# Two half loads of x0 at the heads of the load queues: a change in the first microseconds of a gated attention and FFN kernel

## The chip, the cores and the metric

The kernel runs on 1 core of one Trainium2 chip. The metric is the device time in microseconds (us) of one execution; before the change it is 288.54 us, the median of 3 runs (288.52 to 288.88).

## The reference

For 2048 tokens of width 640 the kernel computes a linear attention branch a and a SwiGLU branch b, and mixes them by a gate of each token. Cut to what matters:

```python
g = sigmoid((x * gate_w).sum(-1, keepdims=True))        # one number for each token
q, k, v = split((x @ wqkv))                             # 32 heads of 20
phi(t) = concat(softmax(t @ w_phi), softmax(-(t @ w_phi)))
kv = sum_s phi(k)[s] outer v[s];  z = sum_s phi(k)[s]
a = ((phi(q) @ kv) / (phi(q) @ z + 1e-6)) @ wo
b = (silu(x @ w_gate) * (x @ w_up)) @ w_down
out = g * a + (1 - g) * b
```

All inputs and the output are bf16.

## The kernel before

The tokens are cut into 16 tiles of 128 (x0 to x15). TensorE needs every x tile transposed, with the 640 features on the partitions in 5 chunks of 128: `xT[:, t, c, :]`. Tiles 0 to 3 are loaded plainly into `xs` and transposed by TensorE; the others are loaded transposed by the DMA engines.

**Two orders written out by hand** drive the build. `LOADS` is the order in which the input DMAs are issued; each has a fixed issuing engine, SP or ACT (ScalarE), and each of the two has a queue of its own that takes them in order. `ORDER` is the order of the work items. The items at the start are:

- `H` (`warm`): a pair of dummy matmuls, 128x128 by 128 columns, on a constant of ones. Nothing reads their results; they wait for no load.
- `X t` (`xpose`): five TensorE transposes of x tile t, and DVE copies of the results into `xT`. For t below 3 there are two copies: chunk 0 (128x128) as soon as the first transpose is done, then chunks 1 to 4 (128x512).
- `G` (`gcol`): TensorE transposes the gate row `gwr` (5 rows of 128) into one column for each chunk, and DVE copies the five columns into column 640 of `wvg`, so that the v matmuls give the gate's dot product as well.
- `U t.c` (`vpart`): the two matmuls (320 and 321 columns) of chunk c of the v projection of tile t, from `xT[:, t, c, :]` and the weight rows `wvg[:, c, :]` (load `w c`). The second one reads column 640, so `U0.0` needs x0's first copy, the weight load w0 and the gate column.
- `V`, `F`, `M`, `K` and so on: the rest. It all follows behind on TensorE in the written order.

Before the change the work starts with thirteen pairs of dummies `H0` to `H12`, then `X0 G X1 U0.0 U1.0 U0.1 X2 U1.1`, and so on. The queues start with: SP: x0, gate row, w1, w2, w3, and the first FFN columns; ACT: w0, x1, x2, x3, w4, and w_phi.

**PSUM** is used as four pairs of banks; `next_pair` takes the least recently used pair that isn't held. An item that writes a pair waits for the reads of what was there.

**Waits** are made by `_Tracker`. For each access it forms keys (space, first byte, end byte) in `keys_of`, and `run` makes an instruction or DMA wait for the last writer and, where it writes, for all readers of every key that overlaps its own, unless its engine is known to have waited already. The key comes from the column part of the access:

```python
        for s in ap.tensor.shape[1:]:
            row *= s
        size = mybir.dt.size(ap.dtype)
        dims = [(step, n) for step, n in list(ap.ap)[1:] if n > 1]
        off = ap.offset % row
```

Here `row` is the number of elements of one partition, and `dims` leaves out the first dimension of the access, which is that of the partitions. Before the change every tile of `xs` is written by one DMA over all 128 partitions. A DMA waits on the engine that issues it; what stands behind it on that engine's queue is issued afterwards.

Of the kernel before, what the change touches and what calls it, by code (L numbers as in the profile page):

```python
# [6 lines left out]
P = 128  # L7
# [23 lines left out]


LOADS = """
x0 w0 x1 g w1 x2 w2 x3 w3 w4 f0 h k0 k1 t4 k2 k3 k4 t5 t6 t7 t8 t9 t10 t11 t12 t13 t14 t15 q0 q1 q2 q3
q4 f1 f2
"""

ORDER = """
H0 H1 H2 H3 H4 H5 H6 H7 H8 H9 H10 H11 H12 X0 G X1 U0.0 U1.0 U0.1 X2 U1.1 U2.0 U0.2 U1.2 U2.1
X3 U2.2 U0.3 U1.3 U2.3 U0.4 U1.4 U2.4 V3 Y F0.1 M1 i3 M0 F0.0 M2 V4 M3 M4 K0 K1 I S0 V6 V5 S1 P0  # L40
K3 K2 P1 E0 V9 K4 E1 S3 V7 P3 K5 S2 V8 V10 S4 P2 P4 E2 R0 E3 K6 S5 P5 S6 i4 E4 V14 K7 K8 P6 V15 S7
R2 E5 K9 S8 P7 R1 E6 K10 S9 V12 P8 E7 P9 K11 S10 P10 F0.2 R3 F1.2 E8 E9 K12 E10 S11 S12 K14 S14
# [11 lines left out]
class _Tracker:  # L54
# [90 lines left out]
    def run(self, eng, fn, reads=(), writes=(), dma=False):  # L145
        rkeys = list(dict.fromkeys(k for a in reads for k in self.keys_of(a)))
        wkeys = list(dict.fromkeys(k for a in writes for k in self.keys_of(a)))
        need = {}

        def req(ev, raw):  # L150
            if ev is None:
                return
            s, v = ev
            if s == eng and not dma and (eng == "pe" or not raw):
                return
            if v > need.get(s, 0):
                need[s] = v

        for k in rkeys:
            for kk in self._conflicts(k):  # L160
                req(self.lastw[kk], True)
                if k[0] == "psum":
                    for s, v in self.readers[kk].items():
                        req((s, v), False)
        for k in wkeys:
            for kk in self._conflicts(k):
                req(self.lastw[kk], True)
                for s, v in self.readers[kk].items():
                    req((s, v), False)
        self._wait(eng, need)  # L170
        ins = fn()
        if dma:
            sn = "d%d" % self.ndma
            self.ndma += 1
            self._add_sem(sn)
            inc = 16
        else:
            sn, inc = eng, 1
        ins.then_inc(self.sem[sn], inc)
        self.cnt[sn] += inc  # L180
        v = self.cnt[sn]
        snap = dict(self.known[eng])
        if not dma:
            snap[sn] = max(snap.get(sn, 0), v)
        self.evknow.setdefault(sn, {})[v] = snap
        ev = (sn, v)
        for k in wkeys:
            self.lastw[k] = ev
            self.readers[k] = {}
        for k in rkeys:  # L190
            r = self.readers[k]
            if r.get(sn, 0) < v:
                r[sn] = v
        return ev


def _build(nc, A_x, A_wqkv, A_w_phi, A_wo, B_x, B_w_gate, B_w_up, B_w_down, gate_w, out):
    tr = _Tracker(nc)
    pe, act, dve, pool, sp = nc.tensor, nc.scalar, nc.vector, nc.gpsimd, nc.sync
# [53 lines left out]
    def at(name, shape, dtype, rel):  # L253
        n = mybir.dt.size(dtype)
        for s in shape[1:]:
            n *= s
        assert rel + n <= SLAB, (name, rel + n, SLAB)
        t = nc.alloc_sbuf_tensor_at(name, list(shape), dtype, offset=sbase + rel)
        tr.reg(t, "sbuf", sbase + rel)
        return t  # L260
# [4 lines left out]
    xs = at("xs", [P, NPE, D], BF16, 10752)  # L265
# [5 lines left out]
    gwr = at("gwr", [P, P], BF16, 30656)  # L271
# [72 lines left out]
    def dma(e, dst, src, transpose=False):  # L344
        eo = tr.eng[e]

        def fn():
            if transpose:
                return eo.dma_start_transpose(dst, src)
            return eo.dma_start(dst, src)  # L350
        rd = [src] if src.tensor.name in tr.base else []
        wr = [dst] if dst.tensor.name in tr.base else []
        return run(e, fn, rd, wr, dma=True)
# [4 lines left out]
            channel_multiplier=cm), [ap], [ap])  # L358


    XQ = ["sp", "act", "act", "act"]
    WQ = ["act", "sp", "sp", "sp", "act"]
    x2 = A_x[0]
    out2 = out[0]

    def load_rows(e, dst, c, c0):
        return dma(e, dst, A_wqkv[c * P:(c + 1) * P, c0:c0 + D])

    def load_x(t):
        dma(XQ[t], xs[:, t, :], x2[t * P:(t + 1) * P, :])  # L370

    def load_xt(t):
        dma("sp", xT[:, t, :, :], x2[t * P:(t + 1) * P, :], transpose=True)
# [7 lines left out]
    def load_wv(c):  # L381
        wv_evs.append(load_rows(WQ[c], wvg[:, c, 0:D], c, 2 * D))

    def load_gate():
        dma("sp", gwr[0:5, :], bass.AP(gate_w.tensor, gate_w.offset, [[P, 5], [1, P]]))

    def load_phi():
        tr._wait("act", dict([wv_evs[3]]))
# [12 lines left out]
    H0 = [0, 6, 12, 19, 25]  # L401
    H1 = [7, 13, 20, 26, 32]
# [342 lines left out]
    def kv_end():  # L745
# [6 lines left out]
        "H": lambda i: warm(), "i": fills, "X": xpose, "G": gcol, "U": vpart, "V": vtile,  # L752
        "M": lambda m: premult(1, m), "R": lambda m: premult(0, m),
        "K": ktile, "S": knorm, "P": kmul, "p": lambda t: kmul(t, "dve"), "E": kvtile, "x": load_x, "t": load_xt, "w": load_wv, "g": load_gate, "h": load_phi, "k": lambda m: load_wt(1, m), "q": lambda m: load_wt(0, m),
        "f": lambda i: load_ffn(FCUT[i], FCUT[i + 1]), "L": load_late_weights, "T": tail_weights, "J": gates,
        "Y": w_blocks, "I": kv_begin, "N": kv_end, "Z": z_row,
# [8 lines left out]
def bass_gated_mix__linear_kernel_hedgehog__swiglu_ffn__prompt_kernel(  # L765
    nc: bass.Bass,
    A_x: bass.AP,
    A_wqkv: bass.AP,
    A_w_phi: bass.AP,
    A_wo: bass.AP,  # L770
    B_x: bass.AP,
    B_w_gate: bass.AP,
    B_w_up: bass.AP,
    B_w_down: bass.AP,
    gate_w: bass.AP,
    out: bass.AP,
):
    _build(nc, A_x, A_wqkv, A_w_phi, A_wo, B_x, B_w_gate, B_w_up, B_w_down, gate_w, out)
# [28 lines left out]
```

## Time and profile before

| | before |
|---|---|
| median of 3 runs | 288.54 us (288.52 to 288.88) |
| the profiled execution | 288.52 us |
| its span, from the first to the last instruction | 287.3 us |
| PE (TensorE matmuls) busy | 284.5 us, 99% |
| PEld (weight loads) busy | 174.7 us, 61% |
| DVE, ACT, POOL busy | 163.4, 151.9, 159.9 us |

The 1.2 us between the profiled execution's time and its span lie outside the instructions. Matmuls are pipelined, so a duration in the profile is one matmul's passage through the array, and the distance between two starts is its cost in a dense stream. "L296" is line 296 of the kernel; the v matmuls, the FFN and the projections are all issued there, the transposes at L308, the dummies at L478, the DVE copies at L320, plain DMAs at L350 and transposing ones at L349. "SPq" and "ACTq" are DMA issues on the two engines; the time of such a row is that of the issue, and the DMA lands later.

### The profile page before, as it was taken

To read this page: it belongs to the slowest core of one execution; us is meant where nothing else is said; L and a number is where in the kernel's file an instruction comes from. 1 tells how busy PE (TensorE), PEld (TensorE's weight loads), DVE (VectorE), ACT (ScalarE), POOL (GpSimd) and SP (SyncE) were. 2 spreads that over 40 slices of the span, in tenths; PEclk is the share of its full clock that TensorE was granted. 3 is DMA by queue.
4 is the path that set the end of the run, shared out by engine and by line. 5 is a ranking of instruction groups with operands and counts; after the bars stand their busy time and mean duration, and the time that the engine had idled before them with its cause. 6 is when DMAs were issued, how large, how long until landed. Compare 5 with 4: busy or idle time off the path is not lost.

```text
span 287.3 us, 4960 instructions
## 1 busy us (share of the span) xinstructions
PE 284.5 (99%) x1975; PEld 174.7 (61%) x1975; DVE 163.4 (57%) x243; ACT 151.9 (53%) x252; POOL 159.9 (56%) x125
## 2 busy tenths in 40 slices
PE   8999999999999999999999999999999999999997
PEld 7667777675644545557775556675554446656776
DVE  2337748576569978589991565970317899000000
ACT  0767778576775566682535653225586552234112
POOL 8286999879446789836542438350754558501000
PEclk9999999999999999999999999999999999999999
DMA  7975797000010598202573002061020006210101
GB/s 236 200 117 120 114 292 257 3 1 2 2 47 0 130 283 162 50 2 50 68 155 73 3 1 50 2 155 37 2 50 0 3 1 123 52 46 0 49 23 48
DMA packets 48944, 21.62 MB, mean 75 GB/s; under 512 B 39384, under 2 KB 48792, under 8 KB 48920
## 3 DMA queue, kind: packets, MB, share of 16 engines
q1 hardware_dynamic: 47400, 20.43, 31.2%
q10 hardware_dynamic: 1520, 0.87, 1.0%
q8 instruction: 16, 0.26, 0.4%
q14 instruction: 8, 0.07, 0.1%
HBM read 9.29 MB, written 2.62 MB: 41 GB/s over the span
## 4 chain that ended last, share of the span: by engine, by line
PE 99%; DVE 0%; issue 0%
PE ps L296 97%; PE ps L478 1%; PE ps L308 1%; DVE osb L733 0%
## 5 line engine op out<-in xcount | busy, mean ns | idle before, releaser
L324 POOL TENSOR_TENSOR hT<-hT,us 128x512 bf16<-128x512 bf16 (+1 forms) x56 | 65.1, 1175 | 65.3 <-DVE hT L328 47.0
L328 DVE SCALAR_TENSOR_TENSOR hT<-hT,ps 128x512 bf16<-128x512 bf16 (+1 forms) x56 | 37.4, 682 | 67.0 <-ACT hT L314 53.3
L296 PE MATMUL ps<-xT,wg 128*128 128x512 bf16 x260 | 64.6, 379 | 0.0
L296 PE MATMUL ps<-xT,wu 128*128 128x512 bf16 x260 | 64.6, 379 | 0.0
L296 PE MATMUL ps<-wd,hT 128*128 128x320 bf16 (+2 forms) x462 | 63.9, 295 | 0.0
L324 POOL TENSOR_TENSOR ph<-eq,qc 128x1320 bf16<-128x1320 bf16 x16 | 42.4, 2648 | 25.6 <-DVE qc L638 20.8
L296 PEld LDWEIGHTS ps<-wd,hT 128*128 128x128 bf16 x462 | 44.5, 98 | 17.4
L296 PE MATMUL ps<-wqk,xT 128*128 128x320 bf16 x320 | 47.7, 299 | 0.0
L314 ACT ACTIVATE hT<-ps 128x512 bf16<-128x512 f32 (+2 forms) x60 | 35.7, 596 | 16.7 <-PE ps L296 16.5
L296 PEld LDWEIGHTS ps<-xT,wu 128*128 128x128 bf16 x260 | 25.4, 98 | 30.7
L314 ACT ACTIVATE us<-ps 128x512 bf16<-128x512 f32 (+1 forms) x56 | 33.5, 598 | 19.2 <-PE ps L296 18.2
L314 ACT ACTIVATE osb<-ps,omg 128x640 bf16<-128x640 f32 (+2 forms) x17 | 12.9, 758 | 55.7 <-PE ps L296 55.7
L296 PEld LDWEIGHTS ps<-xT,wg 128*128 128x128 bf16 x260 | 25.0, 98 | 27.8 <-ACT oT L314 0.8
L324 POOL TENSOR_TENSOR ekr<-ekr,krec 128x1280 bf16<-128x1280 bf16 x16 | 37.4, 2358 | 5.8 <-DVE krec L338 5.8
L296 PEld LDWEIGHTS ps<-wqk,xT 128*128 128x128 bf16 x320 | 30.5, 98 | 13.1 <-issue 0.4
L314 ACT ACTIVATE eq<-ps 128x640 bf16<-128x640 f32 x32 | 22.4, 704 | 20.8 <-POOL ph L324 10.7
L335 DVE TENSOR_REDUCE ksum<-ekr 128x64 f32<-128x1280 bf16 x16 | 23.5, 1470 | 11.7 <-ACT ekr L314 11.7
L314 ACT ACTIVATE ekr<-ps 128x640 bf16<-128x640 f32 x32 | 22.3, 704 | 8.7 <-PE ps L296 8.2
L335 DVE TENSOR_REDUCE qz<-eq 128x64 f32<-128x1280 bf16 x16 | 23.7, 1478 | 2.6 <-ACT eq L314 2.6
L296 PE MATMUL ps<-wog,oT 128*128 128x320 bf16 (+2 forms) x165 | 24.7, 294 | 0.0
L296 PE MATMUL ps<-wvg,xT 128*128 128x320 bf16 (+1 forms) x160 | 24.1, 299 | 0.0
L335 DVE TENSOR_REDUCE qw<-ez 128x64 f32<-128x1280 bf16 x16 | 23.6, 1476 | 0.0
(73 smaller groups left out, 189.4 us busy)
## 6 DMA issues: line engine op xcount, KB each, us to landing
out_dram<-osb SPq DMA_DIRECT2D x15, 160.0 KB, 1.9
wd<-in_B_w_down_dram SPq DMA_DIRECT2D x1, 2080.0 KB, 9.6
wg<-in_B_w_gate_dram SPq DMA_DIRECT2D x1, 1040.0 KB, 10.6
wu<-in_B_w_up_dram SPq DMA_DIRECT2D x1, 1040.0 KB, 12.8
wg<-in_B_w_gate_dram SPq DMA_DIRECT2D x1, 800.0 KB, 5.8
wu<-in_B_w_up_dram SPq DMA_DIRECT2D x1, 800.0 KB, 8.3
wog<-in_A_wo_dram SPq DMA_DIRECT2D x2, 375.0 KB, 7.1
xs<-in_A_x_dram ACTq DMA_DIRECT2D x3, 160.0 KB, 3.6
```

The lines of the kernel that those rows point to most:

```text
L296: last = pe.matmul(o, lhsT=l, rhs=r, start=st, stop=sp_, skip_group_check=sk)
L308: last = pe.transpose(o, i, ident[0:k, 0:k])
L314: return run("act", lambda: act.activation(o, i, func, scale=scale), rd, [o])
L324: return run(e, lambda: eo.tensor_tensor(o, a, b, op), [a, b], [o])
L328: return run("dve", lambda: dve.scalar_tensor_tensor(out=o, in0=a, scalar=s, in1=b, op0=op0, op1=op1), rd, [o])
L335: return run("dve", lambda: dve.tensor_reduce(o, i, AX.X, ALU.add), [i], [o])
L478: last = pe.matmul(bank(2 * pr, 0, P), lhsT=c, rhs=c, start=True, stop=True)
```

## The change

x0 is loaded by two DMAs of 64 rows each, the first issued by SP and the second by ACT, each as the first of its queue. The gate row goes behind the second half on ACT; w0 goes behind the first half on SP. In `ORDER`, the thirteen pairs of dummies in front of `X0` become ten; two pairs stand between `G` and `U0.0`, `X1` follows `U0.0` and no longer precedes it, and one pair stands between `X1` and `U1.0`.

```diff
 LOADS = """
-x0 w0 x1 g w1 x2 w2 x3 w3 w4 f0 h k0 k1 ...
+x0 g w0 x1 w1 x2 w2 x3 w3 w4 f0 h k0 k1 ...
 ORDER = """
-H0 H1 H2 H3 H4 H5 H6 H7 H8 H9 H10 H11 H12 X0 G X1 U0.0 U1.0 U0.1 X2 U1.1 ...
+H0 H1 H2 H3 H4 H5 H6 H7 H8 H9 X0 G H10 H11 U0.0 X1 H12 U1.0 U0.1 X2 U1.1 ...
-    XQ = ["sp", "act", "act", "act"]
-    WQ = ["act", "sp", "sp", "sp", "act"]
+    WQ = ["sp", "sp", "sp", "sp", "act"]
     def load_x(t):
-        dma(XQ[t], xs[:, t, :], x2[t * P:(t + 1) * P, :])
+        parts = [("sp", 0, 64), ("act", 64, P)] if t == 0 else [("act", 0, P)]
+        for e, p0, p1 in parts:
+            dma(e, xs[p0:p1, t, :], x2[t * P + p0:t * P + p1, :])
     def load_gate():
-        dma("sp", gwr[0:5, :], bass.AP(gate_w.tensor, gate_w.offset, [[P, 5], [1, P]]))
+        dma("act", gwr[0:5, :], bass.AP(gate_w.tensor, gate_w.offset, [[P, 5], [1, P]]))
```

More of the change, by code (lines that the diff above doesn't have):

```diff
@@ L33 @@
 LOADS = """
-x0 w0 x1 g w1 x2 w2 x3 w3 w4 f0 h k0 k1 t4 k2 k3 k4 t5 t6 t7 t8 t9 t10 t11 t12 t13 t14 t15 q0 q1 q2 q3
+x0 g w0 x1 w1 x2 w2 x3 w3 w4 f0 h k0 k1 t4 k2 k3 k4 t5 t6 t7 t8 t9 t10 t11 t12 t13 t14 t15 q0 q1 q2 q3
 q4 f1 f2
@@ L38 @@
 ORDER = """
-H0 H1 H2 H3 H4 H5 H6 H7 H8 H9 H10 H11 H12 X0 G X1 U0.0 U1.0 U0.1 X2 U1.1 U2.0 U0.2 U1.2 U2.1
+H0 H1 H2 H3 H4 H5 H6 H7 H8 H9 X0 G H10 H11 U0.0 X1 H12 U1.0 U0.1 X2 U1.1 U2.0 U0.2 U1.2 U2.1
 X3 U2.2 U0.3 U1.3 U2.3 U0.4 U1.4 U2.4 V3 Y F0.1 M1 i3 M0 F0.0 M2 V4 M3 M4 K0 K1 I S0 V6 V5 S1 P0
```

## The prediction

> **What bounds the kernel now.** I read the chain that ended last first, in order of time, because it says where a delay at the start would go.
>
> ```profile
> 12 pieces in order of time: start us, us, what
> 0.84 2.93 PE ps L478 x26
> 3.77 1.32 PE ps L308 x11
> 5.09 0.98 PE ps L296 x6
> 6.08 0.28 PE ps L308 x5
> 6.36 1.37 PE ps L296 x10
> ...
> 77.46 207.92 PE ps L296 x1271
> ```
>
> The chain is TensorE from the first dummy to the last matmul. No later piece is a wait for a load or another engine, so there is no slack behind the start: what the first v matmul loses, the end loses. It also works the other way, so the first 6 us are read instruction by instruction in the timeline:
>
> ```profile
> 0.80 0.40 SPq L350 DMA_DIRECT2D xs<-in_A_x_dram  x1
> 0.82 0.41 ACTq L350 DMA_DIRECT2D wvg<-in_A_wqkv_dram  x1
> 0.84 2.93 PE L478 MATMUL ps<-const-bfloat16-1.0 128*128 128x128 bf16 x26 [0.84 <-PEq L792]
> 1.25 1.42 ACTq L350 DMA_DIRECT2D xs<-in_A_x_dram  x3
> 3.76 0.45 PEld L308 LDWEIGHTS ps<-ident,xs 128*128 128x128 bf16 x5 [0.25 <-DMA xs<-in_A_x_dram]
> 3.76 0.72 PE L308 MATMUL ps<-ident,xs 128*128 128x128 bf16 x5
> 4.53 0.57 PE L308 MATMUL ps<-ident,xs 128*128 128x128 bf16 x5
> 4.86 0.17 DVE L320 COPY wvg<-ps 128x5 bf16<-128x5 bf16 x1
> 5.08 0.66 PEld L296 LDWEIGHTS ps<-wvg,xT 128*128 128x128 bf16 x6 [0.16 <-DVE wvg L320]
> 5.92 0.44 PE L308 MATMUL ps<-ident,xs 128*128 128x128 bf16 x5
> ```
>
> The dummies end as x0 lands (weight loads idle 0.25 us for it). X0 runs at 3.76. Then DVE is the limit: X0's two copies, then the gate column, and U0.0 starts at 5.08, released by that gate copy. So from X0 to U0.0 it is 1.32 us, and X1 (4.53 to 5.10) lies wholly inside that wait. From 5.08 on TensorE is dense. Third, the landing times (KB of each, us from issue to landing), and a duration by tile (minimum, median and maximum in ns):
>
> ```profile
> xs<-in_A_x_dram SPq DMA_DIRECT2D x1, 160.0 KB, 2.9
> xs<-in_A_x_dram ACTq DMA_DIRECT2D x3, 160.0 KB, 3.6
> wph<-in_A_w_phi_dram ACTq DMA_DIRECT2D x1, 25.0 KB, 4.1
> out_dram<-osb ACTq DMA_DIRECT2D x1, 24.0 KB, 1.5
> out_dram<-osb SPq DMA_DIRECT2D x15, 160.0 KB, 1.9
> ```
>
> ```profile
> L308 PE MATMUL ps<-ident,xs x20: 217/219/314, 3.8 to 7.8; 128*128 128x128 bf16 x20
> ```
>
> The last line shows the clock by pace. The five transposes of X0 take 0.72 us, of which 0.31 is the last one's passage: (0.72 - 0.31) / 4 = 0.10 us apart. Those of X2 take 0.44 with a passage of 0.22: 0.055 apart. The dummies are (2.93 - 0.31) / 25 = 0.105 apart. In a closer timeline the step falls inside X1, near 4.8 us, which is 3.96 us after the first dummy at 0.84. The profile's granted clock reads 1.00 over the whole span and doesn't show this slow start; the pace does.
>
> **The change part by part.**
>
> *The second half doesn't start beside the first.* The tracker's key has no partitions: `dims` drops the first dimension and `offset % row` drops the start row. xs[0:64, 0, :] and xs[64:128, 0, :] are therefore the same bytes to it, the second is a write after a write, and ACT waits until SP's half has landed. The built instruction order says so: ACT's first DMA waits for the semaphore of the first DMA. Nothing else stands ahead of it, so behind this wait are queued the second half, the gate row, x1, x2, x3, w4 and w_phi, and X0 (which reads both halves) waits for two landings in a row. This new wait is the main term.
>
> First half: issued at 0.80 as x0 was. Bounds: 1.9 us (a 160 KB store late in the kernel, alone) and 2.9 (x0 itself, twice the rows, with w0 beside it). In the DMA rates from 0.8 to 3.5 us, about 80 KB have moved by 2.7 us and 328 KB by some 3.3, and x0 lands at 3.72, 0.4 later. So I take 2.7 + 0.4, rounded up for an uneven last engine: it lands at 3.2. Second half: issued at 3.2 into an empty ACT queue while SP's queue is full of w0 to w3 and FFN columns. Bounds: 1.5 us (24 KB from ACT at the idle end) and 4.1 (w_phi, an ACT load beside a full SP queue, but of 640 pieces). Nearest is x0's 2.9, the same rows of the same tensor first on its queue; half as many of them, so 2.6. It lands at 5.8, and X0 starts at 5.85 in place of 3.76. U0.0 follows 1.32 later by the same DVE copies: 7.17 in place of 5.08. **+2.09 us.** The gate row is issued about 3.7 and x1 about 4.05 (0.45 and 0.36 an issue). With 2.7 and 3.3 to landing, inside the bounds above, they are there at 6.4 and 7.4, ahead of G at 6.5 and X1 at 7.7 or so. x2, x3 and w4, each some 2.8 us later than before, are also used that much later. On SP, w0 loses 0.4 us of issue and moves 80 KB back, but is wanted 2 us later. All this is put at nothing under the cover of the late X0; if the gate row took w_phi's 4.1 it would land at 7.8 and G, with all behind it, would be 1.3 us later.
>
> *X1 behind U0.0.* In the wait X1 cost nothing; four dummies lie there now (4 x 0.105 = 0.42, free, as they end before the gate copy). X1's 5 x 0.055 and one dummy pair's 2 x 0.055 come onto the path: **+0.39 us** at full pace. The three pairs taken from the front save nothing, since X0 waits for its load. At full pace U1.0 would further wait for X1's first copy: from X2 and its copy that takes 0.55 us (5.92 to 6.47), less the 0.39 that now lie between, 0.16. At half pace the 0.39 are 0.75 and the wait is gone. X2 now takes the PSUM pair that X1 used and waits for X1's second copy, which ends about 0.2 us ahead of it: nothing, and 0.2 more if it were later by as much again.
>
> *The slow start lasts longer.* Ten pairs of dummies are over at 0.84 + 20 x 0.105 = 2.94. TensorE then idles until 5.85, where before it was fed through to the step at 4.8. Bounds: nothing, if the step still comes while TensorE idles, and 3.3 us, if the step came a whole such stretch later than I take it, at 13.77. I count 3.96 us again from X0: step at 9.81. From U0.0 at 7.17 these are 2.64 us at half pace, of which half is lost ((9.81 - 7.17) / 2): **+1.32 us**. I take this because every matmul before the step stands after an unbroken feed in this trace.
>
> [...]
>
> **Sum:** 2.09 + 0.39 + 1.32 = 3.80 us on the profiled execution's 288.52 (span 287.3 and 1.2 around it): 292.3. The median of before is 0.02 above that execution, so **292.3 us**, slower by 1.3%.
>
> **Rivals.** (1) *The clock step comes in time.* The dummies' 2.1 us and X0 at 5.85 might be enough, so that the work from U0.0 on runs at full pace. Then 2.09 + 0.39 + 0.16 = 2.64, 291.2 us. For it: 2.1 of the 3.96 us up to the old step are still fed. Against it: nothing before shows a step after a pause of 2.9 us. (2) *The loads behind the wait are slow.* The second half takes w_phi's 4.1 (7.3) and the gate row about the same: X0 1.5 later, or G 1.3 later, and the sum is near 5.3: 293.8. For it: w_phi is the only row of an ACT load started beside a full SP queue. Against it: its 640 small pieces. (3) *Not slower: the wait is there but costs nothing*, because the halves land as if side by side. Place: ACT's first issue. With X0 at 3.45 (80 KB fewer ahead of each half's end), U0.0 would be at 4.77, 0.31 earlier, and 0.39 + 0.16 come back: +0.24, 288.8, the same. It decides at X0 near 3.9: there the loss is about 0.15 + 0.39, just under 0.2%. The second half would have to land within 0.7 us of its issue, where the shortest landing in the rows above is 1.5. A gain of 0.2% would need X0 at 2.8, when its packets are still moving.
>
> **How the numbers follow.** 0.2% of 288.54 is 0.58 us, about what a measurement of this kernel can tell from no change. Chances: the forecast 0.62, rival 1 0.25, rival 2 0.10, rival 3 0.03. Low end: rival 1 with the second half 0.7 faster (the stores' 1.9) is 290.5. High end: rival 2 at 293.8, and 0.4 for a step that comes later than I take it (0.8 us later, half of it lost). I take 290.5 to 294.2. Rival 3 is left out, and holds nearly all of "same"; faster 0.01, same 0.02, slower 0.97.
>
> **What would show it.** In the changed kernel's profile: ACT's first DMA is issued near 3.2, not 0.8; weight loads idle about 2.9 us for the xs DMA between the dummies and X0; X0 starts near 5.85 and U0.0 1.3 later; X1's and the first v matmuls are spaced at twice the pace of before (0.27 us apart for 320 columns, where 24 of them from 7.84 on take 3.46 us before, 0.14 each) until about 9.8; from there on the same dense stream. If ACT issues its half at 0.8, or X0 starts before 4, the reasoning is wrong at its root; if the pace is full by U0.0, the third term goes; if G waits for the gate row, rival 2 holds.

## The result: slower by 2.7%, and the profile after

The changed kernel takes 296.14 us, the median of 6 runs (295.15 to 299.13), beside 288.71 for the kernel before on the same chip: a ratio of 1.027 (of the means, like all ratios below), with a 95% interval of 1.022 to 1.032. It was forecast slower, at 292.3 us with a range to 294.2; between the medians the loss is 7.4 us and not 3.8. The profiled execution is the fastest of the six: 295.15 us, with a span of 293.9, 6.6 longer than before.

The chain that ended last, in order of time (start, duration, what):

```profile
20 pieces in order of time: start us, us, what
...
0.80 2.23 DMA xs<-in_A_x_dram
...
3.05 0.54 ACTq L350
...
3.63 0.71 ACTq L350
...
4.38 4.77 DMA xs<-in_A_x_dram
...
9.20 0.71 PE ps L308 x5
...
14.66 69.40 PE ps L296 x640
...
84.11 207.92 PE ps L296 x1271
```

Before, this chain was TensorE from 0.84 us on. Now it begins with the landing of x0's first half, goes on with ACT's issues one after another (second half, gate row, x1), and then with a DMA of 4.77 us: the load of x1, not the second half. From 14.66 on the pieces are the same as before (69.40 and 207.92 us); everything was lost ahead of them. In the chain of before the first of these two stands 6.65 us earlier:

```profile
8.01 69.40 PE ps L296 x640
```

The timeline of the same stretch (start, duration, engine and line, and the idle time in front):

```profile
3.05 0.54 ACTq L350 DMA_DIRECT2D xs<-in_A_x_dram  x1
3.63 0.71 ACTq L350 DMA_DIRECT2D gwr<-in_gate_w_dram  x1
4.38 1.43 ACTq L350 DMA_DIRECT2D xs<-in_A_x_dram  x3
6.68 0.72 PE L308 MATMUL ps<-ident,xs 128*128 128x128 bf16 x5 [3.55 <-DMA xs<-in_A_x_dram]
7.46 0.10 PEld L308 LDWEIGHTS ps<-ident,gwr 5*128 5x128 bf16 x1 [0.33 <-DMA gwr<-in_gate_w_dram]
8.01 0.72 PE L296 MATMUL ps<-wvg,xT 128*128 128x320 bf16 x2
9.20 0.71 PE L308 MATMUL ps<-ident,xs 128*128 128x128 bf16 x5 [0.47 <-DMA xs<-in_A_x_dram]
11.07 0.71 PE L308 MATMUL ps<-ident,xs 128*128 128x128 bf16 x5
11.58 2.80 PE L296 MATMUL ps<-wvg,xT 128*128 128x320 bf16 x10
14.22 0.44 PE L308 MATMUL ps<-ident,xs 128*128 128x128 bf16 x5
```

ACT issues its half at 3.05: the wait is there. X0 starts at 6.68 (forecast 5.85), and U0.0 1.32 us later at 8.01, by the same DVE copies as before. X1 could follow at 8.52, when U0.0's second matmul has had its 0.27 us, but starts at 9.20: 0.68 us of wait for x1. The transposes take 0.71 us for five until X2 (11.07) and 0.44 only at X3, at 14.22: the pace stays at half until about 14.2 us, where 9.8 was forecast. G's weight load waited 0.33 us for the gate row, 0.13 more than the 0.20 in front of it before, but U0.0 came no later behind X0 for it.

How long the loads took, from issue to landing (KB of each, median us):

```profile
xs<-in_A_x_dram ACTq DMA_DIRECT2D x3, 160.0 KB, 6.3
...
xs<-in_A_x_dram SPq DMA_DIRECT2D x1, 80.0 KB, 2.2
xs<-in_A_x_dram ACTq DMA_DIRECT2D x1, 80.0 KB, 3.6
```

The two halves are the same size: 2.2 us for the first, 3.6 for the second. x1 to x3 took 6.3 in the median, where the page of before showed 3.6.

### The profile page after: what moved, and what is told of

It reads as the page before. It is cut to its first block, busy times and chain, and to the rows that moved or that the text cites. A ratio compares the mean times of both kernels' runs of the same rounds, so it can differ in the third digit from the quotient of the medians.

```text
span 293.9 us, 4960 instructions
## 1 busy us (share of the span) xinstructions
PE 287.1 (98%) x1975; PEld 175.5 (60%) x1975; DVE 163.4 (56%) x243; ACT 151.9 (52%) x252; POOL 159.7 (54%) x125
## 4 chain that ended last, share of the span: by engine, by line
PE 96%; DMA 2%; ACTq 0%; DVE 0%; issue 0%
PE ps L296 96%; DMA xs<-in_A_x_dram 2%; PE ps L308 1%; ACTq L350 0%; DVE osb L734 0%; PE ps L479 0%
## 5 line engine op out<-in xcount | busy, mean ns | idle before, releaser
L335 DVE TENSOR_REDUCE ksum<-ekr 128x64 f32<-128x1280 bf16 x16 | 23.5, 1470 | 11.7 <-ACT ekr L314 11.7
L296 PE MATMUL ps<-wvg,xT 128*128 128x320 bf16 (+1 forms) x160 | 26.4, 316 | 0.0
```

The source lines that it names most:

```text
L296: last = pe.matmul(o, lhsT=l, rhs=r, start=st, stop=sp_, skip_group_check=sk)
L335: return run("dve", lambda: dve.tensor_reduce(o, i, AX.X, ALU.add), [i], [o])
```

## The experiments

Theory A: the tracker's wait between the halves, which puts all of ACT's loads late, is the cause of all of it. Theory B: the new order, queues and dummies cost a good part by themselves. The chip's median for before was 288.9 to 289.0 us beside these runs.

**The wait taken out.** The key for `xs` also holds the rows:

```diff
+        rows = (0, P)
+        if ap.tensor.name.startswith("xs_"):
+            p0 = ap.offset // row
+            rows = (p0, p0 + list(ap.ap)[0][1])
-            key = (space, lo, hi)
+            key = (space, lo, hi) + rows
```

(and two keys overlap only where their rows do)

> The changed kernel with one edit: the tracker's key for xs also holds the partition rows, so that the two halves of x0 count as different bytes and ACT's first DMA waits for nothing. Theory A (the wait between the halves is the cause of all of it): ACT issues its half at 0.8 us, X0 starts at about 3.4, the pace doubles near 4.8, and the time is 288.8 us, within 0.3 of before. Theory B (the new order, the gate row on ACT and w0 behind x0 cost a good part by themselves): 290 us or more.

Measured: 291.05 us, 1.0083 of before (1.0055 to 1.0110). The halves are issued at 0.80 together and land at 3.11 and 3.43, and X0 starts at 3.52: so far theory A, and about 5 us come back. But 2 us stay, and the pace doubles near 8.7 us. x1, third on ACT behind the gate row, lands at 5.82 (4.26 before), and TensorE stands still for it. Theory A alone fails; part of B holds.

```profile
0.81 0.57 ACTq L355 DMA_DIRECT2D xs<-in_A_x_dram  x1
3.52 0.69 PE L313 MATMUL ps<-ident,xs 128*128 128x128 bf16 x5 [0.38 <-DMA xs<-in_A_x_dram]
5.87 0.72 PE L313 MATMUL ps<-ident,xs 128*128 128x128 bf16 x5 [0.34 <-DMA xs<-in_A_x_dram]
```

**Only the split, with its wait.** The kernel before, with x0 as two halves on SP and ACT and nothing else changed:

> The kernel before with one edit: x0 is split into two halves on SP and ACT with the wait between them; order, dummies and all other loads stay as they were. Theory A: ACT's first issue at 3.0 us, the second half lands near 6.6, w0 and x1 behind it at 7.5 to 9, and the time is 294 to 297 us, about that of the changed kernel. Theory B: under 291 us, since order and queues are the old ones.

Measured: 295.61 us, 1.0232 (1.0216 to 1.0249). The timeline of TensorE:

```profile
6.57 0.72 PE L308 MATMUL ps<-ident,xs 128*128 128x128 bf16 x5 [2.79 <-DMA xs<-in_A_x_dram]
7.21 0.18 PE L308 MATMUL ps<-ident,gwr 5*128 5x5 bf16 x1
10.38 0.72 PE L308 MATMUL ps<-ident,xs 128*128 128x128 bf16 x5 [2.98 <-DMA xs<-in_A_x_dram]
```

The time is as theory A expected; x1 landed at 10.33, later than the 7.5 to 9 expected. Two waits for loads stand here in a row, 2.79 us for x0's second half and 2.98 for x1. The wait is sufficient: the split and its wait alone lose 6.6 us, where the whole change loses 7.4. These 6.6 and the 2 us that stay without the wait don't add up to 7.4, so no share of the loss can be read off them; here w0 stands behind the wait on ACT too, and X1 ahead of U0.0.

**Only the order.** The kernel before with the changed `ORDER`:

> The kernel before with the changed order of items (ten pairs of dummies, X0, G, two pairs, U0.0, X1, one pair, U1.0) and its own loads. Theory A: X0 waits for its load as before (3.7 us); X1's five transposes and a dummy pair come onto the path, with up to 0.16 us of wait for X1's copy: 0.4 to 0.55 us over before, 289.1 to 289.3 us. Theory B: over 290 us.

Measured: 290.24 us, 1.0046 (1.0031 to 1.0062): 1.2 us, more than X1's place can explain. X0 starts at 3.81 as before, but the pace in this profile doubles near 9.3 us. The change has ten pairs of dummies in front of X0, so two kernels part X1's place from the dummies. First, the changed order with thirteen pairs in front:

```diff
-H7 H8 H9 X0 G H10 H11 U0.0 X1 H12 U1.0
+H7 H8 H9 H20 H21 H22 X0 G H10 H11 U0.0 X1 H12 U1.0
```

> The kernel before with the changed order, but thirteen pairs of dummies in front of X0 as before instead of ten (sixteen in all). The order alone with ten pairs lost 1.2 us in the median, and in its profile the pace doubled near 9 us. If that was the pause of 0.7 us in front of X0, the pace doubles near 4.8 us again, and what stays is X1 on the path: 0.4 to 0.55 us over before. If it was X1's place, 1 us or more over before stays.

Measured: 289.29 us, 1.0009 (0.9996 to 1.0021); the pace doubles near 5.9 us. Then the old order with ten pairs:

```diff
-H7 H8 H9 H10 H11 H12 X0 G X1 U0.0
+H7 H8 H9 X0 G X1 U0.0
```

> The kernel before with one edit: ten pairs of dummies in front of X0 instead of thirteen; its order is the old one. X0 waits for its load in both, so by the path nothing changes (0.0 us). If the pause of 0.7 us in front of X0 delays the step to the full pace, the first v matmuls run 0.27 us apart, and 0.5 to 2 us are lost, more in some runs than in others.

Measured: 290.73 us, 1.0054 (1.0036 to 1.0073). So X1's new place costs 0.1% or so, which can't be told from nothing nor from the 0.4 us of the forecast, and three pairs of dummies that compute nothing are worth about 1.7 us between the medians. The profile of the ten pairs:

```profile
0.84 2.29 PE L478 MATMUL ps<-const-bfloat16-1.0 128*128 128x128 bf16 x20 [0.84 <-PEq L792]
3.71 0.72 PE L308 MATMUL ps<-ident,xs 128*128 128x128 bf16 x5 [0.58 <-DMA xs<-in_A_x_dram]
...
7.14 2.59 PE L296 MATMUL ps<-wvg,xT 128*128 128x320 bf16 x10
9.57 0.44 PE L308 MATMUL ps<-ident,xs 128*128 128x128 bf16 x5
```

and of the changed order with thirteen:

```profile
0.84 2.93 PE L478 MATMUL ps<-const-bfloat16-1.0 128*128 128x128 bf16 x26 [0.84 <-PEq L792]
3.83 0.72 PE L308 MATMUL ps<-ident,xs 128*128 128x128 bf16 x5
...
7.13 1.53 PE L296 MATMUL ps<-wvg,xT 128*128 128x320 bf16 x10
```

Ten v matmuls from 7.1 us on take 2.59 us in the one and 1.53 in the other. In the first, a pause of 0.78 us lies between the last dummy (its start and 0.107 us) and X0, in the second 0.25.

**The pause fed.** The changed kernel with 24 more pairs of dummies in front of X0:

> The changed kernel with 24 more pairs of dummies in front of X0, so that TensorE is fed while x0's second half is under way (6.7 us). If the slow start lasts long because TensorE stood idle in that pause, the pace doubles near 4.8 us as before, the v matmuls run 0.14 us apart from the start, and the time falls by about 2.5 us to 292.5 to 293.5, with a smaller spread between runs. If the slow start has another cause (a count from X0, or the late x1), the pace stays at half until 10 to 14 us and the time stays at 295 to 297.

Measured: 295.85 us (294.43 to 297.58), 1.0257 (1.0228 to 1.0285). The pace was full from 4.0 us on, and yet the median is only 0.3 us lower, less than the runs of either kernel differ: the second expectation's time, with the first one's pace. What TensorE waited for (total us, times, longest):

```profile
PEld ps L308 <- DMA xs<-in_A_x_dram: 3.4, 3, 1.7
```

Three times it waited for x loads: x0's second half (landed 7.90 in this run), x1 (9.55) and x2 (11.75). In this profile the half took 4.7 us to land and X0 started 1.27 us later than in the changed kernel's; from X0 to X3 it then took 5.51 us in place of 7.53. So the full pace did save time behind X0, and the loads took it back: the waits for x1 and x2 were 0.77 us at half pace, and weight loads idle 1.7 for them here. Why the half took longer in this run isn't shown.

**SP quiet.** The price of the second half by itself: SP issues nothing more until it has landed:

```diff
-x0 g w0 x1 w1 ...
+x0 s g w0 x1 w1 ...        # s: SP waits for the second half
```

> The changed kernel, with SP holding w0 and all its later loads back until x0's second half has landed, so that this half is alone on the DMA engines. It measures one price: the 3.6 us from ACT's issue to the landing of the second half, where 2.6 were forecast and the first half took 2.2. If the SP queue beside it makes it slow, it lands 1.9 to 2.4 us after its issue, near 5.3 us. If a load from ACT, or the second load of the program, is slow by itself, it stays at 3 us or more. The total is 294 to 299, as all later loads start late.

Landing times in this run, of one execution (293.93 us, just under the 294 to 299 expected):

```profile
xs<-in_A_x_dram ACTq DMA_DIRECT2D x3, 160.0 KB, 2.3
...
xs<-in_A_x_dram SPq DMA_DIRECT2D x1, 80.0 KB, 2.2
xs<-in_A_x_dram ACTq DMA_DIRECT2D x1, 80.0 KB, 2.2
```

Alone, the second half lands 2.2 us after its issue like the first, and x1 to x3, beside which SP starts again only at 5.3 us, in 2.3. The rest, 1.4 us of its 3.6 and 4 of the others' 6.3, comes from what SP has queued beside them. Even with w0 first issued at 5.3 us, this one execution isn't slower than the changed kernel's 295.15 to 299.13.

**The later loads held.** SP holds the first FFN columns, which TensorE needs near 18 us, and the transposing loads behind them, until x2 has landed. First with the 24 pairs, then without:

```diff
-... w3 w4 f0 h k0 k1 ...
+... w3 w4 s f0 h k0 k1 ...   # s: SP waits for x2
```

> The kernel of the fed pause (24 more pairs of dummies), with SP holding the first FFN columns and the transposing loads behind them back until x2 has landed. With the pause fed the pace was full, and TensorE waited for x1 and x2 instead (9.6 and 11.8 us). If those ACT loads are slow because they share the DMA engines with SP's loads for later, x1 lands by 7.5 to 8.0 and x2 by 8.2 to 9.0, and the time falls from 295.9 to 291 to 293. If ACT's loads are slow for their late issue alone, x1 and x2 land within half a us of 9.6 and 11.7 and the time stays at 294 to 297.

> The changed kernel with SP holding the first FFN columns back until x2 has landed, and no dummies added. It is the fourth corner beside the changed kernel (296.1), the fed pause alone (295.9) and both (292.2). If the slow pace and the late loads are two limits side by side, neither edit alone gains much: 294.5 to 296. If the late loads alone were the cause, it falls to 292 to 293 like the run with both.

| changed kernel, median us | f0 at once | f0 held |
|---|---|---|
| pause not fed | 296.14 | 293.42 (292.64 to 294.13) |
| pause fed | 295.85 | 292.15 (291.44 to 292.47) |

With both edits no wait for an x load is left in the profile, and the ratio to before is 1.0099 (1.0074 to 1.0124). x1 and x2 landed at 7.07 and 7.78 us, earlier still than expected; the dummies themselves ran until X0 at 7.42, though its half had landed at 6.84. Holding f0 alone gives 2.7 us, between my two expectations (294.5 to 296, or 292 to 293): x1 to x3 land 3.5 us after their issue, TensorE has no gap after U0.0, and the full pace comes at 10.0 us and not 14.2. Feeding the pause alone gives 0.3, and 1.3 on top of the held f0. So they aren't two equal limits: the late loads are the larger. That they also put off the step to full pace is what the two profiles suggest; the step also lies apart in the two profiles with the pause fed (near 4.0 and 6.5 us), as the last section shows.

```profile
xs<-in_A_x_dram ACTq DMA_DIRECT2D x3, 160.0 KB, 3.5
...
xs<-in_A_x_dram ACTq DMA_DIRECT2D x1, 80.0 KB, 3.5
```

In these lines of the run with f0 held alone the second half still takes 3.5: w0 to w3 beside it are its price. x1 alone took 2.1 with SP quiet, 3.5 here and 4.8 in the changed kernel: of the 2.7 us more, 1.4 come with the weight loads and 1.3 with f0 and the transposes.

**Halves side by side, made better.** Two tries to get a gain out of the idea. One is the kernel without the wait and with thirteen pairs in front of X0; the other has the halves apart, the old order, and the gate row back on SP:

> The kernel with the halves side by side and the changed order and loads, with three more pairs of dummies in front of X0 (thirteen). With ten it lost 2 us: x1, third on ACT, landed at 5.8 us and TensorE waited for it, and the step to full pace came after 8.7. If the pause in front of X0 carries most of it, the median falls to about 290. If x1's late landing carries it, alone or as a second pause that delays the step too, it stays at 290.5 to 291.5.

> What the change seems to aim at, without what the runs so far found to cost: halves of x0 side by side (rows in the tracker's key), the old order with thirteen pairs, the gate row second on SP and x1 second on ACT; w0 is third on SP. X0 starts at 3.5 us in place of 3.8 and U0.0 at 4.8 to 4.9 if w0 has landed, 0.2 us before the old one: 288.5 to 289.0 beside a before of 289.0, which can hardly be told from it. If w0 or x1, pushed back, lands after 5.1, the time is 289.3 to 290.

Measured: 291.15 us, 1.0082 (1.0061 to 1.0103), and 290.08 us, 1.0039 (1.0024 to 1.0054). In the first, the pace was full by X1, but x1 landed at 6.80 and TensorE idled 1.41 us behind U0.0: the three pairs bring nothing while x1 is late. In the second, X0 starts at 3.57 (0.2 earlier than before) but x1, second on ACT, lands at 4.94 in place of 4.26 and w0 at 5.12 in place of 3.91. X1 waits 0.6 us, and the pace doubles only near 8.4. What x0 gains, the next loads lose.

**Two more pairs.** The runs with ten pairs suggested the other direction, on the kernel before:

```diff
-H10 H11 H12 X0 G X1 U0.0
+H10 H11 H12 H13 X0 G X1 H20 U0.0
```

> A version that the runs point to: the kernel before with two more pairs of dummies, one in front of X0 (fourteen) and one between X1 and U0.0, so that TensorE idles less before the step to full pace. The runs with ten pairs lost 1.2 to 1.7 us in the median, and before itself varies from 288.3 to 290.6 between runs. If the idle 0.33 us in its first 4.8 us costs it the step in some runs, the median falls by 0.2 to 0.5 us to 288.5 to 288.8. If thirteen pairs are enough, it stays at 288.9 to 289.2; if fourteen delay X0, it rises by at most 0.1.

Measured: 289.19 us, 1.0008 (0.9998 to 1.0017). No gain, as expected if thirteen pairs are enough. No version here beats the kernel before.

## Why the prediction was wrong, point by point

- **The wait: right.** ACT's first issue came at 3.05 us (forecast 3.2), because the tracker takes the two halves for the same bytes. The run without it loses 2 us in place of 7.4, and the split with its wait alone loses 6.6.
- **"The second half ... 2.6. It lands at 5.8": too short.** It took 3.6, landed at 6.64, and the first term is 6.68 - 3.76 = 2.92 us, not 2.09. The quiet SP queue shows why: 2.2 alone, and with w0 to w3 beside it but f0 held still 3.5. I had put w_phi's 4.1, the one row of an ACT load beside a full SP queue, aside for its small pieces; it was the nearer row.
- **"x1 ... there at ... 7.4 ... All this put at nothing under the cover of the late X0": the step that failed.** I priced x1 at 3.3 from loads issued in the first 2 us, when FFN columns and transposes weren't yet queued. It was issued at 4.38 (the two issues ahead of it took 0.54 and 0.71 us, not 0.45 and 0.36), took 4.77, and landed at 9.15, when X1 could have run at 8.52: 0.68 us, and 0.09 more in front of X2. That the chain of after goes through x1 and not through the second half says more: had the half landed at 5.8 as forecast, and x1 when it did, X1 would still have started at 9.20. With f0 held x1 took 3.5, no wait for it was left, and the kernel took 293.42. Rival 2 had this mechanism, but only for the second half and the gate row. G did wait for the gate row, the sign I gave for that rival, but it cost nothing in front of U0.0.
- **"I count 3.96 us again from X0": wrong rule, and the term was 2.6, not 1.32.** The step came 7.5 us after X0, and it isn't a fixed count from the first matmul either (near 4.0 and 6.5 us in the two runs with the pause fed, behind a first matmul at 0.84 in both; last section). From U0.0 to X3 it is 2.48 us before (5.084 to 7.568) and 6.21 after (8.005 to 14.219). Of the 3.73 more, 0.39 are the moved X1 and dummy pair as forecast, 0.77 the waits for x1 and x2, and 2.57, what is left, the half pace. With X0's 2.92 the sum is 6.65, the 6.6 by which the span grew. Over the forecast's 3.80 that is 2.85 us more: 0.83 for the second half, 0.77 for the x loads that were put at nothing, and 1.25 for the slow pace.
- **X1 behind U0.0, 0.39 us: not refuted.** In the run with the order and thirteen pairs the medians are 0.28 us apart (289.29 and 289.01), and the interval holds both nothing and 0.39.
- **Three dummy pairs "save nothing": right, but they also cost.** In the old order they are worth 1.7 us. In the changed kernel the pause is 3.8 us long, and would be 3.1 with them.

The profiled execution lies 1.0 us under the median of its kernel, and one profile can't show what differs between runs. That the step comes at another moment in each is the likeliest reason, and wasn't tested on this kernel.

## What to carry to other kernels

Before splitting a load over rows, look whether the kernel's own dependency tracking can tell the rows apart; here a false write after write at the head of ACT's queue put its first three issues at 3.05, 3.63 and 4.38 us, where they came at 0.81, 1.41 and 2.25 with the wait taken out. The time from issue to landing wasn't a property of the load (x1 took 2.1, 3.5 and 4.8 us beside different loads): price a load that moves later by a row with the same company in the queues, and follow each load behind it to its first use. Where dummy matmuls keep TensorE fed until its first data arrive, compare the price of fewer with the gain of earlier data: here three pairs fewer cost 1.7 us in the old order, and the halves side by side brought X0 forward by 0.2.

## What the runs showed of the hardware

**The step to full pace came at no fixed time, and earlier with more dummies ahead of X0.** The two kernels with the pause fed start with the same 68 dummies, without a gap from 0.84 us on. In the first (f0 at once) the pace doubles near 4.0 us, in the second (f0 held) near 6.5:

```profile
0.84 5.57 PE L479 MATMUL ps<-const-bfloat16-1.0 128*128 128x128 bf16 x68 [0.84 <-PEq L793]
0.84 6.74 PE L481 MATMUL ps<-const-bfloat16-1.0 128*128 128x128 bf16 x68 [0.84 <-PEq L795]
```

So a count from the first matmul doesn't give the step. For seven other profiles, the time that TensorE stood idle between its first matmul and the step (from the starts of the matmuls, with 0.107 us for 128 columns and 0.267 for 320 at half pace, as they lie apart in the changed kernel's trace):

| run | pace doubles at, us | idle ahead of it, us | of that in front of X0 |
|---|---|---|---|
| before | 4.8 | 0.33 | 0.19 |
| changed order, thirteen pairs | 5.9 | 0.55 | 0.25 |
| the wait taken out, ten pairs | 8.7 | 1.43 | 0.59 |
| old order, ten pairs | 9.3 | 0.97 | 0.78 |
| changed order, ten pairs | 9.3 | 1.18 | 0.88 |
| f0 held, pause not fed | 10.0 | 3.98 | 3.68 |
| changed kernel | 14.2 | 4.82 | 3.76 |

In the changed kernel the rest of the 4.82 us is 0.27 in front of G, 0.68 of wait for x1, and 0.11 in smaller gaps. Four pairs of runs differ in the dummies ahead of X0 alone, and in each the profile with more of them has the earlier step: before and the old order with ten pairs (4.8 and 9.3 us), the changed order with thirteen and ten (5.9 and 9.3), the changed kernel with the pause fed and without (4.0 and 14.2), and the same two with f0 held (6.5 and 10.0). But the idle time doesn't give the moment either: without any the step came near 4.0 and 6.5, and 1.43 us of it stand ahead of 8.7 where 0.97 stand ahead of 9.3. Nor does the pause in front of X0: 3.68 and 3.76 us of it come with steps 4.2 us apart, and with the halves apart and the old order X0 follows the dummies without one, and the step came near 8.4. What sets the moment was not shown.

**Here a load on one engine's queue was slowed by what the other engine had queued.** The same 80 KB from ACT took 2.2 us with SP's queue empty, 3.5 beside w0 to w3 and 3.6 beside SP's whole queue. The core's 16 DMA engines had little room in the changed kernel: over the first 13 us the packets of its two load queues took 57.6% and 29.9% of these engines' span, and their mean busy share, in 40 slices and in tenths, is 80% or more in nearly every slice from 2.9 us on (before: in every slice from 2.6 to 11.7 us):

```profile
DMA  0000002668899988889999899999974999999999
```

**The issue itself got longer.** A half of 64 rows takes 0.57 us to issue where the whole x0 took 0.40, and the gate row behind it 0.71 on ACT where it took 0.36 on SP. With the halves side by side x1, third on ACT behind a half (0.57 us) and the gate row (0.81 there), was issued at 2.25; before, second behind w0 (0.41), at 1.25. Why the issue is longer stays open.
